# A spectral mixing kernel rewritten: d folded at its half-sample centre, the first inverse stage on 32-row array tiles, products left unsummed, one explicit order list

## The chip, the cores and the metric

The kernel runs on one core of one Trainium2 chip. The metric is the device time of one execution in microseconds (us). Each variant was timed in rounds beside the kernel before on the same chip. An execution is called slow when it is more than 1.5% above the fastest one of the same kernel, and "unknown" when there is only one. Engines are named as in the profile: PE multiplies matrices (PEld is its weight load), DVE, ACT and POOL work elementwise, SP only issues transfers. A queue is named after the engine that issues on it.

## The reference, cut to what matters

```python
x = A_x                                              # [1, 2048, 1024], bfloat16
g = sigmoid((x * gate_w).sum(-1, keepdims=True))
a = irfft2(rfft2(x) * (A_w_r + 1j * A_w_i))          # over both axes
b = irfft2(rfft2(x) * (B_w_r + 1j * B_w_i))
return g * a + (1 - g) * b                           # a, b rounded to bfloat16 first
```

Both kernels compute the transforms as matrix products. The sequence axis is split as s = 16*s2 + s1, with 16 values of s1 and 128 of s2. The stages:

- F1 transforms over s2, F2 over d, F3 over s1. The work then falls into 16 units: eight for even columns of the spectrum, eight for odd ones.
- cmul multiplies a unit by the two complex weights.
- I1 is the inverse over s1. Its result is copied from PSUM (the memory that PE writes its results to) into a tile `rl` in SBUF (the on-chip memory that holds all other tiles).
- A **shuffle** moves `rl` by DMA into the exchange buffer `re` (even) or `ro` (odd). It turns pieces that lie on different partitions into long rows on few partitions. It is a transfer from SBUF to SBUF, and no engine can do I2 until all units of its parity have been shuffled.
- I2 (with the gate folded into its weights) and I3 finish the inverse; the even half is kept as `ev` and added to and subtracted from the odd half.

## The kernel before: the parts that matter

```python
def cmul(n):                         # DVE: two products of 2064 columns, then two sums
    ...
    nc.vector.tensor_tensor(p[:, :, :, 0:M], xb, w[:, :, :, 0:M], ALU.mult)      # for r in 0, 1
    ...
    nc.vector.tensor_tensor(Y[:, 0, :, 0:M], p1[:, :, 0, 0:M], p2[:, :, 1, 0:M], ALU.subtract)
    nc.vector.tensor_tensor(Y[:, 1, :, 0:M], p1[:, :, 1, 0:M], p2[:, :, 0, 0:M], ALU.add)

def i1(n, r):                        # PE: 64-row tiles, one PSUM tile per r
    ...
    for k in range(2):
        w = ((0, 2), (1, 0))[r][k]
        for tt in range(2):
            for jh in range(2):
                hin = hp(jh ^ tt)
                nc.tensor.matmul(ps[hp(jh), tt * 512:(tt + 1) * 512], lhsT=WI[hin, 2 * u + tt, w, :],
                                 rhs=Y[hin, k, 2 * tt:2 * tt + 2, o:o + 256], start=(k == 0), stop=(k == 1))
    ...                              # rl has 4 buffers
    nc.scalar.copy(out=rl[:, :, r, :], in_=ps[:].rearrange("p (t m) -> p t m", t=2))
    if r == 1:
        for tt in range(2):          # the shuffle: 128 partitions -> 8 partitions, 256 KB
            t = 2 * u + tt
            p0 = 32 * (t // 4) + t % 4
            nc.gpsimd.dma_start(RR[par][p0:p0 + 29:4, :, :], rl[:, tt].rearrange("p r m -> p (r m)"))
```

All 32 shuffles go on the POOL queue, which carries nothing else. The main loop issues F2 of unit n, I1 of unit n-3, F3 and cmul of unit n-1, and lets I2 and I3 of the even half begin in its last turns.

Of the kernel before, what the change touches and what calls it, by code (L numbers as in the profile page):

```python
# [20 lines left out]
WID = (257, 256)  # L21
PIT = (258, 256)
# [25 lines left out]

def make_constants():
# [3 lines left out]
    E = np.zeros((NT, 2, 2, 2, 128))  # L53
    EZ = np.zeros((NT, 2, 2, 2, 128))
    for t in range(NT):
        for j, k2 in enumerate(quad_reps(t)):
            th = 2 * np.pi * s2 * k2 / 128
            F[:, t, j // 2, 0, j % 2] = np.cos(th)
            F[:, t, j // 2, 1, j % 2] = -np.sin(th)
            E[t, j // 2, 0, j % 2] = np.cos(th)  # L60
            E[t, j // 2, 1, j % 2] = np.sin(th)
            EZ[t, j // 2, 0, j % 2] = 2 * np.cos(th)
            EZ[t, j // 2, 1, j % 2] = -2 * np.sin(th)
            if k2 == 0:
                F[:, t, j // 2, 1, j % 2] = np.cos(np.pi * s2)
                E[t, j // 2, 1, j % 2] = np.cos(np.pi * s2)
                EZ[t, j // 2, 0, j % 2] = 1
                EZ[t, j // 2, 1, j % 2] = np.cos(np.pi * s2)
    F = F.reshape(128, 128)
    c["F1"] = _bf16np(np.concatenate([F, -F], axis=1))  # L70
    c["E"] = _bf16np(E.reshape(4, 4, 8, 128).transpose(0, 2, 1, 3).reshape(128, 128))
    c["EZ"] = _bf16np(EZ.reshape(128, 128) / 128)
    d1 = np.arange(512)
    i = np.arange(256)
    FD = np.zeros((512, 2, 2, 256))
    IG = np.zeros((2, 2, 256, 512))
    for eo in range(2):
        m = 2 * i + eo
        ph = 2 * np.pi * np.outer(d1, m) / D
        FD[:, eo, 0] = np.cos(ph)  # L80
        IG[eo, 0] = 2 * np.cos(ph).T
        if eo == 0:
            IG[0, 0, 0] = 1
        m = 2 * i + (2 if eo == 0 else 1)
        ph = 2 * np.pi * np.outer(d1, m) / D
        FD[:, eo, 1] = -np.sin(ph)
        IG[eo, 1] = -2 * np.sin(ph).T
        if eo == 0:
            FD[:, 0, 1, 255] = np.cos(np.pi * d1)
            IG[0, 1, 255] = np.cos(np.pi * d1)  # L90
    IG /= S * D
    c["FD"] = _bf16np(FD.reshape(4, 128, 2, 512).transpose(1, 2, 0, 3))
    c["IG"] = _bf16np(IG.reshape(2, 2, 2, 128, 512).transpose(3, 0, 1, 2, 4).reshape(128, 8, 512))
    s1 = np.arange(NS1)
    WF = np.zeros((128, NT, 3, 64))
    WI = np.zeros((128, NT, 3, 64))
    for t in range(NT):
        for jh in range(2):
# [4 lines left out]
            for p in range(64):  # L103
                w = np.exp(-2j * np.pi * k[p] * s1 / S)
                kk = k[p] % 128
                if kk in (0, 64):
                    cc = 0 if kk == 0 else 1
                    al[:, cc, 0, p] = w
                    be[cc, 0, :, p] = w.conj()
                    continue  # L110
                eps = 1 if kk in reps else -1
                j = reps.index(kk if eps > 0 else 128 - kk)
                al[:, 0, j, p] = w
                al[:, 1, j, p] = 1j * eps * w
                be[0, j, :, p] = w.conj()
                be[1, j, :, p] = 1j * eps * w.conj()
            al = al.reshape(64, 64)
            be = be.reshape(64, 64).T
            h = slice(64 * jh, 64 * jh + 64)
            WF[h, t, 0], WF[h, t, 1], WF[h, t, 2] = al.real, al.imag, -al.imag  # L120
            h = h if t % 2 == 0 else slice(64 - 64 * jh, 128 - 64 * jh)
            WI[h, t, 0], WI[h, t, 1], WI[h, t, 2] = be.real, be.imag, -be.imag
    c["WF"] = _bf16np(WF)
    c["WI"] = _bf16np(WI)
# [4 lines left out]
def gated_mix(ctx, tc, x_in, we_in, wo_in, gw_in, out):  # L129
# [3 lines left out]
    xv = x_in.flatten_outer_dims().rearrange("(s2 s1) d -> s2 s1 d", s1=NS1)  # L133
# [5 lines left out]
    wp = ctx.enter_context(tc.tile_pool(name="wp", bufs=1))  # L139
    wk = ctx.enter_context(tc.tile_pool(name="wk", bufs=2))  # L140
    pp = ctx.enter_context(tc.tile_pool(name="pp", bufs=3, space=bass.MemoryType.PSUM))
    pl_pool = tc.alloc_tile_pool(name="plp", bufs=1, space=bass.MemoryType.PSUM)
# [4 lines left out]
    def ptile():  # L147
        return pp.tile([P, 1024], F32, name="pt", tag="pt")

    ctx.enter_context(tc.manual_schedule())  # L150
    warm = const.tile([P, 512], BF16, name="warm")
    nc.vector.memset(warm[:], 0.0)
    wps = ptile()
    for _ in range(6):
        nc.tensor.matmul(wps[:, 0:512], lhsT=warm[:, 0:128], rhs=warm[:], start=True, stop=True)  # L155
    F1 = const.tile([P, 2, 128], BF16, name="f1")
    nc.scalar.dma_start(F1[:].rearrange("p a b -> p (a b)"), dr["F1"])
    gws = const.tile([P, 8], BF16, name="gws")
    nc.scalar.dma_start(gws[:], gw_in)
    Re = big.tile([P, 16 * 1024], BF16, name="re")  # L160
    Ro = big.tile([P, 16 * 1024], BF16, name="ro")
    x = Re[:].rearrange("p (s d) -> p s d", s=NS1)
    for s0, n in ((0, 1), (1, 1), (2, 2), (4, 2), (6, 2), (8, 2), (10, 2), (12, 2), (14, 2)):
        nc.sync.dma_start(x[:, s0:s0 + n, :], xv[:, s0:s0 + n, :])
    FD = const.tile([P, 2, 4, 512], BF16, name="fd")
    WF = const.tile([P, NT, 3, 64], BF16, name="wf")
    WI = const.tile([P, NT, 3, 64], BF16, name="wi")
    IG = const.tile([P, 8, 512], BF16, name="ig")
    Ec = const.tile([P, 128], BF16, name="ec")
    Ez = const.tile([P, 128], BF16, name="ez")  # L170

    y = big.tile([P, 4, 2, 2 * NT, NS1, 4], BF16, name="y")
    Ws = {}
    wt = [wp.tile([P, 2064], BF16, name=f"w{k}", tag=f"w{k}") for k in range(4)]

    def load_w(n):
        par, u = n // NU, n % NU
        if n < 4 or 8 <= n < 12:
            w = wt[n % 4][:]
        elif n < 8:  # L180
            w = Ro[:, (n - 4) * 2064:(n - 3) * 2064]
        else:
            w = y[:, n - 12, 0].rearrange("p t s c -> p (t s c)")
        w = w[:, 0:8 * PIT[par]].rearrange("p (t a m) -> p t a m", t=2, a=4)
        nc.sync.dma_start(w, w_in[par][u])
        Ws[n] = w

    nc.sync.dma_start(FD[:, 0], dr["FD"][:, 0])
    nc.sync.dma_start(WF[:, 0:4], dr["WF"][:, 0:4])
    load_w(0)  # L190
    nc.sync.dma_start(Ez[:], dr["EZ"])
    nc.sync.dma_start(WI[:, 0:4], dr["WI"][:, 0:4])
    load_w(1)
    nc.sync.dma_start(WF[:, 4:16], dr["WF"][:, 4:16])
    load_w(2)
    nc.sync.dma_start(WI[:, 4:16], dr["WI"][:, 4:16])
    nc.sync.dma_start(Ec[:], dr["E"])
    for n in range(3, 8):
        load_w(n)
    nc.sync.dma_start(FD[:, 1], dr["FD"][:, 1])  # L200
    nc.sync.dma_start(IG[:], dr["IG"])

    gwz = const.tile([P, 8, 32], BF16, name="gwz")
    nc.gpsimd.memset(gwz[:], 0.0)
    gh = const.tile([P, 8], F32, name="gh")
    junk = const.tile([P, 8], F32, name="junk")
    nc.scalar.activation(junk[:], gwz[:, 0, 0:8], ACT.Sigmoid)
    nc.vector.tensor_scalar(gh[:], gws[:], 0.5, None, ALU.mult)
    gq = gwz[:].rearrange("p (q e) c -> p q e c", e=2)
    nc.vector.tensor_tensor(gq[:, :, 0, 0], gh[:, 0:4], gh[:, 4:8], ALU.add)  # L210
    nc.vector.tensor_tensor(gq[:, :, 1, 0], gh[:, 0:4], gh[:, 4:8], ALU.subtract)

    yo = y[:].rearrange("p q e t s c -> p (q e t) s c")
    for s1 in range(NS1):
        ps = ptile()
        for q in range(4):
            for h in range(2):
                nc.tensor.matmul(ps[:, q * 256:(q + 1) * 256],  # L218
                                 lhsT=x[:, s1, h * 512 + q * 128:h * 512 + (q + 1) * 128],
                                 rhs=(bc(F1[:, 0, :]).to_broadcast([P, 2, 128]) if h == 0 else F1[:]), start=(h == 0), stop=(h == 1))  # L220
        i_ = ps[:].rearrange("p (a c) -> p a c", c=4)
        if s1 == 15:
            for e, cp in ((0, nc.scalar.copy), (1, nc.vector.tensor_copy)):
                cp(out=y[:, :, e, :, s1, :], in_=ps[:].rearrange("p (q e t c) -> p q e t c", q=4, e=2, c=4)[:, :, e])
        elif s1 % 2 == 1:
            nc.vector.tensor_copy(out=yo[:, :, s1, :], in_=i_)  # L226
        else:
            nc.scalar.copy(out=yo[:, :, s1, :], in_=i_)  # L228

    RR = [r[:].rearrange("p (s f) -> p s f", s=NS1) for r in (Re, Ro)]  # L230
    EV = Re[:].bitcast(F32).rearrange("p (s f) -> p s f", s=NS1)
    EA = const.tile([P, NS1, 128], BF16, name="ea")
    EB = const.tile([P, NS1, 128], BF16, name="eb")
    zt = const.tile([P, NS1], BF16, name="zt")

    def gate_hat():
        ps = ptile()
        for e in range(2):
            for q in range(4):
# [154 lines left out]
    for n in range(12):  # L394
        f2(n)
        if n == 0:
            gate_hat()
# [89 lines left out]
```

## Time and profile before

The median of the runs beside the changed kernel was 145.0 us (144.06 to 148.08 in 4 runs).

| | PE | DVE | ACT | POOL | granted PE clock |
|---|---|---|---|---|---|
| busy us of 144.4 | 121.9 | 97.6 | 93.3 | 19.6 | 0.961 |

Busy time of each engine by stretch (start:end, length, then busy time of PE, PEld, DVE, ACT, POOL, PE clock, DMA share, GB/s):

```profile
42.00:69.00 27.00, 23.57 (x279) 10.90 (x276) 26.14 (x33) 25.81 (x28) 8.06 (x14) 1.00 0.94 241
102.00:136.20 34.20, 32.40 (x300) 20.60 (x302) 21.01 (x20) 15.06 (x16) 2.37 (x4) 1.00 0.33 114
```

The mixed stage is held by DVE and ACT (26.14 and 25.81 of 27 us), the last one by PE (32.40 of 34.20 us).

### The profile page before, as it was taken

To read this page: it belongs to the slowest core of one execution; us is meant where nothing else is said; L and a number is where in the kernel's file an instruction comes from. 1 tells how busy PE (TensorE), PEld (TensorE's weight loads), DVE (VectorE), ACT (ScalarE), POOL (GpSimd) and SP (SyncE) were. 2 spreads that over 40 slices of the span, in tenths; PEclk is the share of its full clock that TensorE was granted. 3 is DMA by queue.
4 is the path that set the end of the run, shared out by engine and by line. 5 is a ranking of instruction groups with operands and counts; after the bars stand their busy time and mean duration, and the time that the engine had idled before them with its cause. 6 is when DMAs were issued, how large, how long until landed. Compare 5 with 4: busy or idle time off the path is not lost.

```text
span 144.4 us, 2878 instructions
## 1 busy us (share of the span) xinstructions
PE 121.9 (84%) x1188; PEld 68.1 (47%) x1206; DVE 97.6 (68%) x113; ACT 93.3 (65%) x97; POOL 19.6 (14%) x37
## 2 busy tenths in 40 slices
PE   6999979929899898888867999868869999999910
PEld 2688844416344443334324345433455665756500
DVE  0177740089279999999999279599433456898990
ACT  4255546665699999999995899997935244253200
POOL 1000000000033222233333033033330000000000
PEclk9999999975799999999999999999999999999985
DMA  4999999968716999999865315527464000464553
GB/s 148 298 361 419 406 411 405 415 244 284 297 14 168 240 279 278 353 250 202 163 139 133 126 18 140 131 43 168 110 166 110 0 0 0 167 253 166 208 228 145
DMA packets 11088, 29.19 MB, mean 202 GB/s; under 512 B 3781, under 2 KB 4165, under 8 KB 10949
## 3 DMA queue, kind: packets, MB, share of 16 engines
q1 hardware_dynamic: 6048, 20.55, 38.3%
q0 software_dynamic: 4608, 8.41, 24.8%
q8 instruction: 9, 0.15, 0.5%
q10 hardware_dynamic: 420, 0.07, 0.3%
q14 instruction: 3, 0.02, 0.0%
HBM read 16.42 MB, written 4.19 MB: 143 GB/s over the span
## 4 chain that ended last, share of the span: by engine, by line
PE 55%; ACT 24%; DMA 9%; issue 4%; DVE 2%; another core or an unknown queue 2%; DVEq 1%; POOL 0%; ACTq 0%; POOLq 0%
PE pt L378 18%; PE pt L218 10%; PE pt L275 10%; ACT rl L349 10%; PE pv L367 9%; DMA re<-rl 5%; DMA zt<-zs 4%; ACT X L310 4%; ACT T L279 3%; PE pt L344 3%; ACT V L370 2%; PE pt L155 2%; ACT zs L245 2%; DVE ot L390 2%
## 5 line engine op out<-in xcount | busy, mean ns | idle before, releaser
L275 PE MATMUL pt<-fd,y 128*128 128x512 bf16 x117 | 30.5, 394 | 3.8 <-ACT rl L349 2.6
L349 ACT CAST rl<-pt 128x1024 bf16<-128x1024 f32 x32 | 32.9, 1038 | 0.0
L378 PE MATMUL pt<-ig,V 128*128 128x512 bf16 x121 | 29.6, 379 | 1.1 <-ACT V L370 0.7
L370 ACT CAST V<-pv 128x1024 bf16<-128x1024 f32 x16 | 16.3, 1021 | 19.2 <-PE pv L367 19.2
L344 PE MATMUL pt<-Y,wi 64*64 64x512 bf16 x256 | 20.1, 387 | 3.8 <-ACT T L279 0.8
L275 PEld LDWEIGHTS <-y 128*128 128x128 bf16 x128 | 12.6, 100 | 20.3 <-issue 8.6
L279 ACT CAST T<-pt 128x1024 bf16<-128x1024 f32 x16 | 16.3, 1017 | 8.3 <-PE pt L275 4.1
L378 PEld LDWEIGHTS <-V 128*128 128x128 bf16 x128 | 11.7, 98 | 13.9 <-ACT V L370 1.9
L354 POOL DMA_DIRECT2D re<-rl x16 | 9.6, 606 | 59.8 <-ACT rl L349 59.8
L310 ACT CAST X<-pt 128x1024 bf16<-128x1024 f32 x16 | 16.5, 1033 | 0.0
L218 PE MATMUL pt<-f_84,re 128*128 128x256 bf16 x128 | 15.6, 289 | 0.0
L218 PEld LDWEIGHTS <-re 128*128 128x128 bf16 x128 | 13.0, 103 | 3.1 <-DMA re<-in_x_dram 0.8
L228 ACT CAST y<-pt 128x1024 bf16<-128x1024 f32 x8 | 8.1, 1013 | 8.4 <-PE pt L218 8.4
L354 POOL DMA_DIRECT2D ro<-rl x16 | 9.5, 596 | 26.4 <-ACT rl L349 26.4
L386 DVE COPY re<-pt 128x1024 f32<-128x1024 f32 x5 | 6.1, 1225 | 10.2 <-PE pt L378 10.2
L226 DVE CAST y<-pt 128x1024 bf16<-128x1024 f32 x7 | 8.6, 1225 | 5.2 <-PE pt L218 5.2
L344 PEld LDWEIGHTS <-wi 64*64 64x64 bf16 x256 | 6.4, 106 | 11.9 <-issue 10.7
L389 DVE TENSOR_TENSOR ot<-pt,re 128x1024 bf16<-128x1024 f32 x8 | 9.8, 1224 | 3.0 <-PE pt L378 3.0
L367 PE MATMUL pv<-ea,re 128*128 128x128 bf16 x64 | 8.1, 219 | 2.9 <-DMA re<-rl 1.7
L295 PE MATMUL pt<-T,wf 64*64 64x512 bf16 (+2 forms) x192 | 9.8, 307 | 0.4 <-ACT T L279 0.3
L367 PEld LDWEIGHTS <-re 128*128 128x128 bf16 x128 | 7.5, 98 | 5.4 <-issue 2.5
L390 DVE TENSOR_TENSOR ot<-re,pt 128x1024 bf16<-128x1024 f32 x8 | 9.7, 1210 | 0.0
(96 smaller groups left out, 128.2 us busy)
## 6 DMA issues: line engine op xcount, KB each, us to landing
re<-rl POOLq DMA_DIRECT2D x16, 256.0 KB, 8.0
ro<-rl POOLq DMA_DIRECT2D x16, 256.0 KB, 5.1
out_dram<-ot SPq DMA_DIRECT2D x8, 512.0 KB, 2.6
re<-in_x_dram SPq DMA_DIRECT2D x7, 512.0 KB, 8.6
ro<-in_we_dram SPq DMA_DIRECT2D x4, 516.0 KB, 8.0
y<-in_wo_dram SPq DMA_DIRECT2D x4, 512.0 KB, 6.5
fd<-cst_fd SPq DMA_DIRECT2D x2, 512.0 KB, 9.1
ig<-cst_ig SPq DMA_DIRECT2D x1, 1024.0 KB
```

The source lines that it names most:

```text
L218: nc.tensor.matmul(ps[:, q * 256:(q + 1) * 256], lhsT=x[:, s1, h * 512 + q * 128:h * 512 + (q + 1) * 128], rhs=(bc(F1[:, 0, :]).to_broadca ...
L275: nc.tensor.matmul(ps[:, tt * 512:(tt + 1) * 512], lhsT=y[:, q, par, 2 * t:2 * t + 2, :, :].rearrange("p j s c -> p (j s c)"), rhs=FD[:, p ...
L279: nc.scalar.copy(out=T[:].rearrange("p a b -> p (a b)"), in_=ps[:])
L295: nc.tensor.matmul(ps[ho, tt * 512 + dst:tt * 512 + dst + ln], lhsT=WF[hp(jh), 2 * u + tt, w, :], rhs=T[hp(jh), tt, src:src + ln], start=( ...
L310: nc.scalar.copy(out=xo, in_=ps[:].rearrange("p (t r m) -> p t r m", t=2, r=2))
L344: nc.tensor.matmul(ps[hp(jh), tt * 512:(tt + 1) * 512], lhsT=WI[hin, 2 * u + tt, w, :], rhs=Y[hin, k, 2 * tt:2 * tt + 2, o:o + 256], start ...
L349: nc.scalar.copy(out=rl[:, :, r, :], in_=ps[:].rearrange("p (t m) -> p t m", t=2))
L354: nc.gpsimd.dma_start(RR[par][p0:p0 + 29:4, :, :], rl[:, tt].rearrange("p r m -> p (r m)"))
L367: nc.tensor.matmul(ps[:, s * 512 + ch * 128:s * 512 + ch * 128 + 128], lhsT=RR[par][:, s1, c0 + 256 * ab:c0 + 256 * ab + 128], rhs=Ew[:, s ...
L370: nc.scalar.copy(out=V[:].rearrange("p s c k -> p (s c k)"), in_=ps[:])
L378: nc.tensor.matmul(ps[:, s * 512:(s + 1) * 512], lhsT=V[:, s, ch, :], rhs=IG[:, par * 4 + ch, :], start=(ch == 0), stop=(ch == 3))
L390: nc.vector.tensor_tensor(ot[:, :, 1, :], ev, pv, ALU.subtract)
```

## The change

The intent: halve the columns of F2 by folding d about its half-sample centre (columns j and 1023-j), take two DVE sums per unit away by letting I1 add up all four products, spread copies over the engines, and give every engine a fixed instruction order. The diff replaces almost the whole kernel. Its core, with cuts marked:

```diff
 # F1: instead of one eviction, a copy and two folds per s1
-    nc.scalar.copy(out=yo[:, :, s1, :], in_=i_)
+    cp(e, t..., ps[:, 512:1024]...)                                  # ACT
+    for v, op in enumerate((ALU.add, ALU.subtract)):                  # DVE, or POOL for eight
+        Q[e].tensor_tensor(yo[:, v, k:k + n, s1, :], a..., b..., op)
 # F2: half the columns
-    for q in range(4): matmul(ps[:, tt*512:(tt+1)*512], lhsT=y[...], rhs=FD[:, par, q, :])
+    for v in range(2):
+        for b in range(2): matmul(ps[:, tt*512+v*256:tt*512+v*256+256], lhsT=y[...], rhs=FD[:, par, v, b, :])
 # cmul: no sums
-    nc.vector.tensor_tensor(Y[:, 0, ...], p1[...], p2[...], ALU.subtract)
-    nc.vector.tensor_tensor(Y[:, 1, ...], p1[...], p2[...], ALU.add)
 # I1: 32 input rows per tile; row groups j of 32 go to separate PSUM banks
+    mm = [(0,0,0,lo,256), (64,1,1,lo,256), (128,0,1,lo,256), (128,1,0,lo,256)]   # even units: 4 tiny ones more
+    for q, (w, ri, wi, a, b) in enumerate(mm):
+        for tt in range(2):
+            for H in range(2):
+                for j in range(2):
+                    r = slice(64*H + 32*j, 64*H + 32*j + 32)
+                    lh = C["WJ"][r, 2*u + tt, w:w + 64]
+                    o = pss[tt][hp(H ^ tt), j*512:(j+1)*512]...
+                    nc.tensor.matmul(o[:, :, a:b], lhsT=lh, rhs=src[r, ri, wi, tt, :, a:b], ...)
 # shuffle: twice as many, half as large, to 4 partitions each
-    nc.gpsimd.dma_start(RR[par][p0:p0+29:4, :, :], rl[:, tt]...)
+    for j in range(2):
+        Q[q].dma_start((Re, Ro)[par][p0+4*j:p0+4*j+25:8, :], rl[:, tt, j, :])
 # order list (one token an instruction group; H is a shuffle, its last letter the queue, S is SP, P is POOL)
+ ... R:3:1:A W:S:11 H:0:0:S R:1:0:A R:1:1:D F3:5:0 W:S:7 ... H:0:1:P F2:6:3 X:4:A ...
+ ... X:14:A H:15:1:P J:12:0:1 VC:0:5:A ... H:13:1:P ... H:12:0:S VC:0:4:A H:15:0:S J:14:0:1 H:12:1:P ...
 # also: eleven rl evictions and some others on DVE, three of the sixteen I3 groups (two even, one odd) in half, POOL fixes column 0
```

I1 sums over 32 rows at a time, so the two row groups j are different outputs. The diff puts them in two PSUM banks of the same 64 partitions. A unit's `rl` therefore holds, on its partitions, 4 exchange rows x 32 pieces (16 values of s1, real and imaginary) instead of 8 rows x 16 pieces. The same 8.4 MB are now moved by 64 shuffles of 128 KB to 4 partitions each, in runs of 1 KB, instead of 32 of 256 KB to 8 partitions, in runs of 2 KB. Half of them go on the SP queue.

## The prediction, as it was put on record

> What bounds the kernel now. No engine bounds the whole span; the page's totals are PE 121.9 us, DVE 97.6, ACT 93.3, POOL 19.6 of 144.4. By windows four stages differ. To 18.6 us the forward transform over s2 streams on PE. From 18.6 to 42 us the pipeline fills badly: DVE is busy 10.2 of 23.4 us, the chain of waits goes through the gate (2.3 us zs copy, 5.8 us zt transfer), and the PE clock falls to 0.66 in 30:40. From 42 to 69 us DVE is 97% and ACT 96% busy. From 102 to 136.2 us PE is 95% busy with I2 (16 matmuls, 0.89 us) and I3 (8 matmuls, 1.73 us).
>
> Removed.
> 1. Half of F2: 128 matmuls of 512 columns (8 take 1.89 us in the chain) become 256 columns: estimate 30 -> 14 us of PE.
> 2. The two sums of cmul: 32 DVE operations of 0.69 us, 22 us. I1 now accumulates the four products on PE.
> 3. Half of I3 for three of sixteen units, 2.6 us of PE.
>
> Added.
> 1. A fold at F1: instead of 16 evictions of 1.0 to 1.2 us, ACT copies to SBUF and DVE (or POOL, for eight) adds and subtracts. From 0.69 us for 512 and 1.22 us for 1024 elements I estimate 0.43 us for 256; DVE pays 32 of them, 13.7 us. Eight odd halves fold on PE (+3.5 us).
> 2. I1 in 32-row tiles: the same 2048 streamed columns per unit, but 32 matmuls instead of 16; even units add 32 tiny ones. Before, 8 matmuls on 64-row tiles took 0.56 us and 8 one-column ones 0.21 us. If eight concurrent tiles stream like four, I1 costs 18 + 7 us. This is the least certain term.
> 3. Eleven rl, three V, two T and two X evictions move to DVE; fixes, folds and odd sums go to POOL. The Trainium skill, "GPSIMD Engine Reference", section "Performance versus the Vector engine", puts a two-input POOL add at about twice the VectorE time (4497 against 2293 ns for 2048 elements); nothing in before checks it.
>
> Sums (estimates, counts times these durations): PE about 107, DVE 104, ACT 89. ACT plus DVE stays near 191: the 22 us saved are spent on the fold. So the gain is PE work and overlap. Even halves of F1 come first, so F2, F3 and products should start near 14 to 18 us; more even I2/I3 units fill PE in the mixed stage. After the last I1, before still has 12 I2 and 13 I3 groups and an 8 us tail (42 us); after has 10 I2, 7 whole and 3 half I3, 24 us, plus some 8 us of bubble and tail.
>
> By stage: 17 us of F1, 72 us mixed, 32 us last: 121; with stalls 123 us. It should be 115 to 132. Chances: faster by over 2% 0.95, within 2% 0.03, slower 0.02. Nearly all of it is critical, since the chain alternates between engines.
>
> What would show it. Page: PE near 107, DVE 104, ACT 89. Groups: F2 near 0.11 us per matmul streamed, no sums after the products, folds near 0.43 us. Windows: DVE over 80% busy from 20 to 45 us, clock at 1.0; about 32 us after the last rl eviction. The zt transfer no longer in the chain.
>
> What would make it wrong. If 32-row tiles don't run concurrently, I1 costs up to twice as much: +15 us. If DVE's products hold up POOL (the skill's "SBUF — State Buffer" says the two share a port pair, exclusively), fixes and shuffles come late and I1 waits. A strict order with four fixed PSUM buffers may stall every engine on one late copy. The odd shuffles may leave a bubble over 5 us before the last stage.

## More of the kernel before

Weight loads and stores go on the SP queue.

The page of the profiled execution begins with busy time per engine, then shows the span in 40 slices of 3.6 us (a digit is the busy share in tenths):

```profile
span 144.4 us, 2878 instructions
PE 121.9 (84%) x1188; PEld 68.1 (47%) x1206; DVE 97.6 (68%) x113; ACT 93.3 (65%) x97; POOL 19.6 (14%) x37
...
PE   6999979929899898888867999868869999999910
DVE  0177740089279999999999279599433456898990
...
PEclk9999999975799999999999999999999999999985
...
L275 PE MATMUL pt<-fd,y 128*128 128x512 bf16 x117 | 30.5, 394 | 3.8 <-ACT rl L349 2.6
L344 PE MATMUL pt<-Y,wi 64*64 64x512 bf16 x256 | 20.1, 387 | 3.8 <-ACT T L279 0.8
...
re<-rl POOLq DMA_DIRECT2D x16, 256.0 KB, 8.0
ro<-rl POOLq DMA_DIRECT2D x16, 256.0 KB, 5.1
```

In the group lines the numbers are busy time, the mean of one instruction in ns, and idle time just before with what ended most of it. L275 is F2, L344 is I1. The last two lines are the shuffles: 256 KB each, 8.0 and 5.1 us in the median from issue to landing.

PE has one longer gap, near 30 us (the digit 2 in its row), and otherwise only short ones.

## The result, and the profile after

The result is correct and slower: 170.8 us in the median (169.52 to 172.66 in 4 runs) against 145.0 us. The ratio is 1.175 (95% interval 1.161 to 1.189). Ratios in this document are the mean time of one kernel's fast runs over that of the other's fast runs of the same rounds, so not quite the ratio of the medians quoted. The page after:

```profile
span 169.7 us, 4270 instructions
PE 120.6 (71%) x1814; PEld 81.9 (48%) x1814; DVE 99.7 (59%) x119; ACT 82.7 (49%) x104; POOL 56.2 (33%) x85
...
PE   7499999959895396733303998999702779999710
DVE  0558849777939839602820097796002416879791
...
PEclk9969999999999569995555699999965558999995
...
L507 PE MATMUL pt<-p,wj 32*64 32x510 bf16 (+2 forms) x768 | 22.2, 338 | 10.1 <-ACT rl L208 4.6
...
L436 PE MATMUL pt<-fd,y 128*128 128x256 bf16 x128 | 16.8, 282 | 2.0 <-DVE rl L210 2.0
...
re<-rl POOLq DMA_DIRECT2D x16, 128.0 KB, 8.2
...
ro<-rl POOLq DMA_DIRECT2D x16, 128.0 KB, 8.3
```

Set against the lines of before: of the three engines costed only PE has more work than was predicted, and no engine's is near the span. F2 (L436) has fallen from 30.5 to 16.8 us. I1 (L507) takes 22.2 us for all units. But a shuffle of half the size now lands in 8.2 or 8.3 us, and PE has holes: five slices in the middle with digits 3, 3, 3, 0 and 3, and two later with 0 and 2. The granted clock falls to 0.5 in and after those holes, so part of PE's 120.6 us is work at a lower clock. The windows of the holes, columns as above:

```profile
70.00:80.00 10.00, 3.91 (x60) 1.81 (x60) 2.39 (x3) 5.15 (x6) 1.37 (x2) 0.81 0.71 154
80.00:90.00 10.00, 1.50 (x24) 0.44 (x23) 5.30 (x5) 2.02 (x2) 2.73 (x4) 0.50 0.81 210
...
120.00:130.00 10.00, 1.86 (x16) 0.66 (x8) 1.23 (x1) 1.52 (x2) 0.38 (x1) 0.70 0.46 116
```

In these 30 us PE works 7.3 us. The other engines idle for most of it too. What they wait for (engine, line, what it waited for: us in total, times, longest):

```profile
ACT rl L208 <- DMA re<-rl: 10.4, 3, 4.3
...
DVE rl L210 <- DMA ro<-rl: 10.3, 1, 10.3
...
ACT rl L208 <- DMA ro<-rl: 8.8, 1, 8.8
...
DVE p L479 <- DMA wx<-in_wo_dram: 7.6, 1, 7.6
...
PE pt L533 <- DMA ig<-cst_ig: 8.4, 1, 8.4
```

Copies into `rl` wait for shuffles out of `rl` (its four buffers are all in transit), products wait for a weight load, and the first I2 (L533) waits for a transfer. The profile puts that last wait down to the load of the `ig` table, which I2 does not read. By the trace's packet records (my own count) the table's last packet ended at 94.3 us, after I2 had begun at 91.8; the last 1 KB packet of the even shuffles on SP ended at 90.1 us, and the semaphore of that shuffle was complete at 91.2. I2 waited for the shuffles. The SP queue's own timeline shows why (start, length, instruction, count):

```profile
44.27 17.88 SPq L522 DMA_DIRECT2D re<-rl  x8
62.26 2.93 SPq L278 DMA_DIRECT2D y<-in_wo_dram  x1
65.23 0.89 SPq L278 DMA_DIRECT2D wx<-in_wo_dram  x1
66.22 14.69 SPq L522 DMA_DIRECT2D re<-rl  x6
80.96 1.31 SPq L266 DMA_DIRECT2D ig<-cst_ig  x1
82.32 1.61 SPq L278 DMA_DIRECT2D y<-in_wo_dram  x3
98.11 32.53 SPq L522 DMA_DIRECT2D ro<-rl  x16
```

The lengths of rows with several shuffles hold the waits between them too. The six from 66.22 us stand back to back and take 14.69 us, 2.4 us for each 128 KB. One issue alone takes 0.53 us when little is on its way on SP, and up to 6.24 us when several transfers are. What holds it the profile does not name. It is not the transfer eight before, for which each issue has to wait in this program: by the landings in the trace, that one had landed at least 2.6 us before each issue of over 1 us after 40 us began. The weight loads stand in line among them: `wx` at 65 us, for which DVE waits 7.6 us, and the last three at 82 us.

I counted the packet records of this trace and of a variant of the kernel before with its shuffles on SP (e4_before_sp below). Where the 4-row shuffles run alone on SP, 4.3 packets of 1 KB are in flight, 46 ns each, so about 90 GB/s. With 8-row shuffles at most 8.3 packets of 2 KB are in flight, 84 ns each, so about 200 GB/s. The size of the packets is not what makes the difference: 1 KB in 46 ns and 2 KB in 84 ns are nearly the same rate. All this is on SP. On POOL the packets are of 4 KB in all kernels that I counted, and no limit of four shows: with several shuffles outstanding, 4-row ones have 6 to 9 packets in flight (e1 below, stretches of 3 us after 72 us), 8-row ones 7 to 12 (e13 below).

The figures on SP are what the Trainium skill says to expect: the page "DMA: Bandwidth & Descriptors", section "Why a DMA increments its semaphore by 16 and not by 1", states that a transfer is given the largest number of DMA engines, up to 16, that divides the size of the slowest dimension on both sides. Four destination rows allow four engines, eight rows eight. The traces agree with it on SP, at 4.3 and 8.3 packets in flight; for POOL no run here shows it. The prediction did not use it.

### The profile page after: what moved, and what is told of

Its sections match the earlier page's. It is cut to its first block, busy times and chain, and to the rows that moved or that the text cites. A ratio compares the mean times of both kernels' runs of the same rounds, so it can differ in the third digit from the quotient of the medians.

```text
span 169.7 us, 4270 instructions
## 1 busy us (share of the span) xinstructions
PE 120.6 (71%) x1814; PEld 81.9 (48%) x1814; DVE 99.7 (59%) x119; ACT 82.7 (49%) x104; POOL 56.2 (33%) x85
## 5 line engine op out<-in xcount | busy, mean ns | idle before, releaser
L208 ACT CAST rl<-pt 128x1024 bf16<-128x1024 f32 x21 | 20.8, 1017 | 25.7 <-DMA re<-rl 10.4
L507 PE MATMUL pt<-p,wj 32*64 32x510 bf16 (+2 forms) x768 | 22.2, 338 | 10.1 <-ACT rl L208 4.6
L210 DVE CAST rl<-pt 128x1024 bf16<-128x1024 f32 x11 | 13.4, 1223 | 25.6 <-PE pt L507 14.0
L208 ACT CAST V<-pt 128x1024 bf16<-128x1024 f32 x13 | 13.2, 1016 | 25.7 <-PE pt L533 25.7
L533 PE MATMUL pt<-ea,re 128*128 128x128 bf16 x64 | 11.1, 266 | 18.8 <-ACT re L208 9.1
L479 DVE TENSOR_TENSOR p<-X,ro 128x2048 bf16<-128x2048 bf16 x16 | 20.1, 1302 | 5.8 <-DMA ro<-in_we_dram 2.9
L507 PEld LDWEIGHTS <-wj 32*64 32x64 bf16 x768 | 12.3, 111 | 18.8 <-issue 16.0
L533 PEld LDWEIGHTS <-re 128*128 128x128 bf16 x128 | 10.2, 123 | 21.5 <-issue 9.9
L377 POOL TENSOR_TENSOR y<-wx 128x256 bf16<-128x256 f32 x16 | 14.1, 908 | 15.8 <-ACT wx L208 8.8
L436 PE MATMUL pt<-fd,y 128*128 128x256 bf16 x128 | 16.8, 282 | 2.0 <-DVE rl L210 2.0
L208 ACT COPY wx<-pt 128x256 f32<-128x256 f32 (+1 forms) x25 | 11.3, 459 | 14.1 <-PE pt L332 8.6
L332 PE MATMUL pt<-f,re 128*128 128x128 bf16 x192 | 14.3, 237 | 2.6 <-DMA re<-in_x_dram 2.4
L436 PEld LDWEIGHTS <-y 128*128 128x128 bf16 x128 | 12.1, 100 | 5.5 <-issue 4.0
```

The lines of the kernel that those rows point to most:

```text
L208: nc.scalar.copy(out=out, in_=in_)
L210: Q[e].tensor_copy(out=out, in_=in_)
L332: nc.tensor.matmul(o, lhsT=lh, rhs=rh, start=(h == 0), stop=(h == 1))
L377: Q[e].tensor_tensor(yo[:, v, k:k + n, s1, :], a.rearrange("p (k c) -> p k c", c=4), b.rearrange("p (k c) -> p k c", c=4), op)
L436: nc.tensor.matmul(ps[:, tt * 512 + v * 256:tt * 512 + v * 256 + 256], lhsT=y[:, v, par, b, 2 * t:2 * t + 2, :, :].rearrange("p j s c -> p ...
L479: nc.vector.tensor_tensor(p[:, r], xb, w, ALU.mult)
```

## The experiments

Theories, in the order in which they came up:

- **A**: the SP queue is what hurts; shuffles there are slow and hold up the loads.
- **B**: too few `rl` buffers.
- **C**: too many transfers, whatever their form.
- **D**: the strict order list stalls the engines on each other, whatever the transfers do.
- **E**: a burst of weight loads takes the DMA bandwidth from the shuffles.
- **F**: the form of the shuffle (4 rows, 1 KB runs) that the 32-row tiling brings makes it slow on either queue, worse on SP.

B could not be tried alone, as more `rl` buffers did not fit into SBUF. Two others could not be built: one shuffle for both row groups, and one with 16 pieces as the slowest dimension of both sides, which by the rule above would have put 16 engines to work with all else kept.

### All shuffles on one queue

e1_all_pool puts all 64 on POOL, e2_all_sp all on SP:

```diff
-... H:0:0:S ... H:3:0:S ... H:15:0:S ...
+... H:0:0:P ... H:3:0:P ... H:15:0:P ...      # e1; e2 has :S for all
```

> Edit: the 32 shuffles that stand on the SP queue go to the POOL queue; nothing else moves. Theory A (the SP queue carries a shuffle with 4 destination partitions on only about 4 of 16 DMA engines, 88 packets of 1 KB per us, so each takes 1.5 to 2 us of a queue that also carries the weights and the I3 table): the idle stretches at 73 to 92 us and 121 to 130 us go, the time falls to 128 to 140 us. Rival B (four rl buffers are too few for a landing of 8 us, on any queue): the POOL landings are 8 us as well, so 160 us or more. Rival C (halved shuffles, 64 of 128 KB in place of 32 of 256 KB, are too many transfers): with all 64 on one software queue, 170 us or more.

> Edit: all 64 shuffles on the SP queue, which doubles the suspected cost. Theory A: 64 shuffles of 128 packets at 88 packets per us are 93 us of transfer in series, between about 40 us and the last 30 us of work, so 185 to 210 us. Rivals B and C: near 170 us.

Measured: e1 163.78 us (161.44 to 165.34, two fast and two slow), ratio to before 1.109 (1.095 to 1.123); e2 186.99 us (one run, state unknown). Both correct. So the SP queue does cost: some 16 us more with all on it, and 7 us (by medians) to 10 us (by ratios to before) less with none. But most of the loss stays without it, and A, which foretold 128 to 140 us, is only part of the answer. The forecast that e1 meets is B's (160 us or more); but too few buffers and too slow a landing are the same wait, which this run does not separate. e1's POOL queue has waits of its own (profile of a slow run, 164.4 us; start, length, instruction, count, idle before and what ended it):

```profile
65.26 0.69 POOL L522 DMA_DIRECT2D re<-rl  x1 [1.69 <-DMA re<-rl]
67.81 0.69 POOL L522 DMA_DIRECT2D re<-rl  x1 [1.86 <-DMA re<-rl]
70.20 0.69 POOL L522 DMA_DIRECT2D re<-rl  x1 [1.69 <-DMA re<-rl]
```

Here each does wait for the shuffle eight before it, which by the trace had landed 0.3 to 0.6 us before (at 65.0, 67.3 and 69.9 us): one issue per 2.4 us, with POOL's fixes for I1 behind them. There are six such waits, 10.1 us in all. With 32 shuffles of 256 KB on POOL, in the kernel before and in e13 below, there are none.

### One row per transfer

e3_row_dmas cuts every shuffle on SP into four of one row, 32 KB, to give the parts to the queue separately:

```diff
-        Q[q].dma_start((Re, Ro)[par][p0+4*j:p0+4*j+25:8, :], rl[:, tt, j, :])
+        for i in range(4):                                   # on SP only
+            Q[q].dma_start((Re, Ro)[par][p0+4*j+8*i:p0+4*j+8*i+1, :], rl[32*i:32*i+32, tt, j, :])
```

> Edit: the 32 shuffles stay on the SP queue, but each is issued as four, one per destination partition, with 32 pieces of 1 KB outermost: same bytes, same packets, four times as many transfers (128). Theory A with its mechanism (the outermost count of 4 confines a transfer to 4 engines): packets in flight rise from 4.3 to about 16, the stalls go, 128 to 142 us, the DMA share rises where shuffles run alone. If it is the SP queue as such (issue cost per transfer, in order), not the engine count: more transfers make it worse, 180 us or more. Rival C too: worse than 170 us.

Measured: 191.52 us (190.63 to 192.69), ratio 1.309 (1.297 to 1.322), correct. This run did not test what it was made for. SP became the limit by issuing:

```profile
105.19 44.94 SPq L524 DMA_DIRECT2D ro<-rl  x57
```

That is 0.79 us per transfer with the waits between them (one issue takes 0.59 us in the median), with about 3 packets in flight by my count. What follows is only that cutting transfers smaller is worse; it says nothing about the number of DMA engines.

### The shuffles' bytes taken away

e7_tiny_shuffle keeps every instruction and its order but moves 4 KB in each shuffle instead of 128 KB. Its output is wrong, which doesn't matter for the time.

```diff
-        Q[q].dma_start((Re, Ro)[par][p0+4*j:p0+4*j+25:8, :], rl[:, tt, j, :])
+        Q[q].dma_start((Re, Ro)[par][p0+4*j:p0+4*j+25:8, 0:512], rl[0:97:32, tt, j, :])
```

> Edit to the changed kernel: every shuffle stays where it is, on its queue, but moves 4 KB (one 1 KB piece to each of its 4 partitions) instead of 128 KB; the result is wrong on purpose. Theory A' (moving the shuffles' bytes to 4 partitions a time is what the lost time is): the stalls at rl, V and the late loads go and the time is 120 to 133 us, near the prediction. Rival D (the strict order list over four PSUM buffers stalls the engines by itself, whatever the transfers do): 150 us or more.

Measured: 130.42 us (130.03 to 130.72), ratio 0.891 (0.884 to 0.898). From the page of this run:

```profile
PE 110.6 (86%) x1814; PEld 75.3 (58%) x1814; DVE 99.6 (77%) x119; ACT 81.8 (63%) x104; POOL 53.1 (41%) x85
...
PE   6969999999779799779989989999969999996500
...
PEclk9999999999999999999999999999999999999995
```

No holes, a full clock, and a time inside the predicted range (115 to 132). So D falls as a cause by itself: with the same order list and the same 64 transfers, what costs 40 us (170.8 against 130.4) is what the shuffles carry, and how. PE's busy time falls by 10 us because the clock stays up. C, as a matter of the bare count, falls too.

### The loads as rivals

e8_pool_tinyloads is e1 with the last four weight loads cut to 1/16 (wrong); e9_pool_loads_act is e1 with the late loads on the ACT queue.

```diff
 # e8
-        Q[q].dma_start(w, w_in[n // NU][n % NU])
+        Q[q].dma_start(w[:, 0:128], w_in[n // NU][n % NU][:, 0:128])        # for n >= 12
 # e9
-... W:S:10 ... W:S:11 ... W:S:9 ... W:S:15 ... c:S:IG ...
+... W:A:10 ... W:A:11 ... W:A:9 ... W:A:15 ... c:A:IG ...
```

> Edit to the kernel with all shuffles on POOL: the last four weight loads move 32 KB instead of 512 KB (wrong result on purpose), which takes 2 MB from the burst at 47 to 70 us. Theory E (with the SP queue freed, these loads go out in one burst and the shuffles wait behind them in the DMA engines): 142 to 155 us, the shuffles' median landing well below 7.1 us. If the burst is no matter: 160 us or more.

> Edit to the kernel with all shuffles on POOL: the eight late weight loads and the I3 table are issued from the ACT queue at their places in the order list, so that they are spread in time again instead of going out together. Theory E: 145 to 157 us. If contention with loads is no matter: 160 us or more.

Measured: e8 159.79 us and e9 173.55 us, one run each, state unknown, where e1 took 163.78 (161.44 and 163.17 in its fast runs). The bytes of those four loads are worth 4 us at most, and spreading loads to ACT made it worse. This does not rule E out as a part of e1's loss: in e8 too the DMA engines are full from 50 to 60 us (share 1.05) while PE works 2.51 of 10 us. E falls as the main cause because e13 below, with all of these loads and the shuffles on POOL, takes 149.66 us: its DMA engines are as full (share 0.99 from 45 to 66 us), and PE still works 16.05 of these 21 us.

### The kernel before with the shuffles' form and queue changed

Three kernels put one property of the new shuffles into the old kernel. e4_before_sp only changes the queue. e10_before_split cuts each 8-row shuffle into two of 4 rows, 128 KB, one unit half on SP and one on POOL, as the changed kernel has them. e11_before_split_pool has the same cut, all on POOL.

```diff
 # e4
-                nc.gpsimd.dma_start(RR[par][p0:p0+29:4, :, :], rl[:, tt]...)
+                nc.sync.dma_start(RR[par][p0:p0+29:4, :, :], rl[:, tt]...)
 # e10 (e11: nc.gpsimd for both)
-                nc.gpsimd.dma_start(RR[par][p0:p0+29:4, :, :], rl[:, tt]...)
+                for h in range(2):
+                    (nc.sync, nc.gpsimd)[tt].dma_start(RR[par][p0+16*h:p0+16*h+13:4, :, :], rl[64*h:64*h+64, tt]...)
```

> Edit to the kernel before: its 32 shuffles (8 destination partitions, 256 KB, runs of 2 KB) move from the POOL to the SP queue, behind and between the loads. If the SP queue's in-order issue is what hurts, in any kernel: 152 to 175 us. If only the four-partition form does: within 3% of the kernel before.

> Edit to the kernel before: each of its 32 shuffles of 256 KB to 8 partitions becomes two of 128 KB to 4 partitions; those of one half of each unit stand on the SP queue, the others on POOL, as in the changed kernel. Nothing else of the change is in it. Theory F (a shuffle to 4 partitions runs on only 4 DMA engines, so it lands late and holds its rl buffer and its queue, whatever the compute around it): 155 us or more. Rival G (the loss needs the changed kernel's order list or its other transfers): within 3% of the kernel before.

> The same split of the kernel before with all 64 halves on the POOL queue. Theory F: 150 to 165 us, landings of 6 us or more for 128 KB in the quiet odd stage, where 256 KB took 5.1 us. Rival G: within 3%.

| shuffles in the kernel before | us | before, same rounds | |
|---|---|---|---|
| 8 rows, SP (e4) | 147.88, one run | 146.16 | +1.2% |
| 4 rows, POOL (e11) | 150.94, one run | 147.17 | +2.6% |
| 4 rows, half SP, half POOL (e10) | 156.67, its one fast run of four | 147.17 | +6.5% |

All are correct. Three of e10's four runs were slow (160.98 to 163.1 us) and are left out of the table. Neither the SP queue alone nor the 4-row form alone hurts the old kernel much; together they cost it some 10 us, by one fast run. And it gets the same hole as the changed kernel, here in a window and in the wait that ends it (the profile is of a slow run, 160.98 us):

```profile
80.00:90.00 10.00, 1.61 (x16) 1.64 (x17) 2.15 (x3) 0.00 (x0) 0.91 (x2) 0.52 0.50 160
...
PE pv L369 <- DMA ro<-rl: 12.5, 1, 12.5
```

The profile names an odd shuffle as what ended the wait, again by the last event. By the trace the last even shuffle on SP landed at 87.7 us, 0.7 us before I2 began at 88.4. Before that, SP did wait for the transfer eight before: seven issues in a row, from 71.09 to 84.52 us, began within 0.1 us of its landing. e10's pieces are of 4 rows with runs of 2 KB, and on SP at most 4.2 of them are in flight, so it is the 4 rows and not the shorter runs that make a shuffle slow there. For POOL e11 decides nothing: 150.94 us lies in F's range (150 to 165) and in the rival's (within 3%). Its landing times are a miss of my expectation, as the median of the odd ones is 4.5 us and not 6 or more; POOL waited for earlier shuffles eight times, 11.0 us in all, where it never does in the kernel before.

### The changed kernel with 8-row shuffles

e12_eight_rows keeps the whole rewrite but gives I1 32 x 32 tiles: real and imaginary go to separate banks, the row groups j to separate partitions. Then `rl` again holds 8 rows, and one 256 KB shuffle replaces two. e13_eight_rows_pool has all 32 on POOL.

```diff
-                        lh = C["WJ"][r, 2*u + tt, w:w + 64]
-                        o = pss[tt][hp(H ^ tt), j*512:(j+1)*512]...
+                            lh = C["WJ"][r, 2*u + tt, w:w + 32]              # one pass per c (re, im)
+                            q0 = 64*(H ^ tt) + 32*j
+                            o = pss[tt][q0:q0+32, c*512:(c+1)*512]...
...
-        for j in range(2):
-            Q[q].dma_start((Re, Ro)[par][p0+4*j:p0+4*j+25:8, :], rl[:, tt, j, :])
+        Q[q].dma_start((Re, Ro)[par][p0:p0+29:4, :], rl[:, tt].rearrange("p j m -> p (j m)"))
```

> Edit to the changed kernel: I1 runs on 32-row by 32-column array tiles, real and imaginary parts in separate PSUM banks, so that one half unit again fills 8 rows by 16 samples and is shuffled in one transfer of 256 KB to 8 partitions, on the same queue and place as before (32 transfers instead of 64); everything else stays. PE pays: 64 matmuls of 512 columns per odd unit instead of 32. Theory F: 132 to 150 us, at most 8.3 packets in flight where SP shuffles run alone, and PE becomes the limit again. Rival: the 4-row form is not what costs, so 168 us or more, as PE work only grew.

> The same with all 32 shuffles on the POOL queue. Theory F: 132 to 150 us, near the run with both queues; a quiet-stage landing near 5 us as in the kernel before.

Measured: e12 149.33 us (147.91 to 149.76), ratio 1.013 (1.004 to 1.022), neither faster nor slower by 2%; e13 149.66 us (one run). Both correct. With 8 rows the queue no longer matters, and 21 us of the loss are gone, although PE has more to do:

```profile
PE 126.3 (86%) x2318; PEld 83.4 (57%) x2326; DVE 99.6 (68%) x119; ACT 82.7 (56%) x104; POOL 43.7 (30%) x69
...
L511 PE MATMUL pt<-p,wj 32*32 32x510 bf16 (+2 forms) x1280 | 34.6, 343 | 3.2 <-issue 1.3
...
re<-rl POOLq DMA_DIRECT2D x8, 256.0 KB, 5.9
```

A shuffle twice as large lands in 5.9 us where it took 8.2. I1 costs 34.6 us instead of 22.2. This shows that the form of the shuffle (F) is what costs most, and what was against changing it: the form that makes the shuffle quick makes I1 slow. e12 changes three things of the form at once, 8 rows for 4, runs of 2 KB for 1 KB and 32 transfers for 64. Against the number alone speaks e7 (64 transfers, 130.42 us), against the runs alone e10.

e17_eight_rows_tiny takes the bytes of e12's shuffles away (16 KB each, wrong), to split what is left:

```diff
-        Q[q].dma_start((Re, Ro)[par][p0:p0+29:4, :], rl[:, tt].rearrange("p j m -> p (j m)"))
+        Q[q].dma_start((Re, Ro)[par][p0:p0+29:4, 0:1024], rl[0:113:16, tt].rearrange("p j m -> p (j m)"))
```

> Edit to the version with 32x32 tiles and 8-row shuffles: each shuffle moves 16 KB instead of 256 KB (wrong result on purpose). If the PE work of those tiles is what holds that version at 149 us: 142 to 149 us. If the shuffles still cost: 130 to 138 us.

Measured: 139.06 us, one run, between the two forecasts: both costs are there. Of the 19 us between e12 and e7, about 9 us (139.1 - 130.4) go with the form of I1, and about 10 us (149.3 - 139.1) with the bytes of 8-row shuffles.

### The unsummed products undone

e14_summed keeps the rewrite but sums the products on DVE again, in place, so that I1 can run on 64-row tiles with 8-row shuffles. e15_summed_act also moves eight `rl` copies from DVE to ACT.

```diff
+    def sums(n):
+        p = Ps[int(n)][:].rearrange("p r t (a w) m -> p r w (t a) m", w=2)
+        for k, op in ((0, ALU.subtract), (1, ALU.add)):
+            nc.vector.tensor_tensor(p[:, 0, k], p[:, 0, k], p[:, 1, 1 - k], op)
...
-                            lh = C["WJ"][r, 2*u + tt, w:w + 32]
+                        ... lhsT=C["WJ"][hp(H), 2*u + tt, w:w + 64], rhs=src[hp(H), ri, wi, tt, :, a:b]
 # e15 besides
-... R:0:0:D ... R:3:0:D ... R:5:0:D ...
+... R:0:0:A ... R:3:0:A ... R:5:0:A ...
```

> Edit to the changed kernel: I1's part of the change is undone and all the rest kept: the products are summed on DVE again (in place, 32 operations of 0.69 us, +22 us of DVE), I1 runs on 64-row tiles with 16 matmuls per unit, and so each shuffle is one of 256 KB to 8 partitions; same order list. If the 4-row shuffle forced by the 32-row tiles is what failed: 135 to 146 us, DVE near 121 us busy and the limit. If something else in the rewrite costs: 155 us or more.

> The same, with 8 of the 11 rl evictions that the order list gives to DVE moved to ACT (DVE about 112 us, ACT about 91). If DVE is the limit there: 3 to 8 us less than without. If the strict order or PE is: the same within 2%.

Measured: e14 152.4 us (151.23 to 153.22), ratio 1.054 (1.037 to 1.071), between its two forecasts; e15 154.93 us (152.52 to 156.87; one fast run, 152.52, and three slow), no gain and a miss. Both correct. Now DVE binds: 120.6 us busy in e14, and full over 50 us:

```profile
30.00:80.00 50.00, 35.52 (x549) 22.37 (x546) 48.03 (x56) 32.82 (x36) 18.52 (x27) 0.85 0.59 172
```

So, for all units at once, leaving the products unsummed was worth having (e12 has 1.013): the fold has taken the room on DVE that the sums would need. For the odd units alone this is not shown: the mixture below has sums there and came out no slower, but changes the order list too.

### A mixture

e18_mixed runs even units as in e12 and odd units as in e14, with the last I1 ahead of two even I3 groups. e19_mixed_act also moves three odd `rl` copies and one V copy from DVE to ACT.

```diff
 # e18
+    even units: 32 x 32 tiles, products unsummed; odd units: sums on DVE, 64-row tiles
-... U:0:5:2 R:12:1:A H:12:0:S VC:0:4:A H:15:0:S J:14:0:1 H:12:1:P U:0:4:3 R:14:0:A R:14:1:D E:5:A H:14:0:S H:14:1:P ...
+... the same without U:0:5 and U:0:4, which now stand after the last J and H
 # e19 besides
-... R:11:0:D ... R:8:1:D ... VC:0:3:D ... R:13:1:D ...
+... R:11:0:A ... R:8:1:A ... VC:0:3:A ... R:13:1:A ...
```

> Edit to the changed kernel: 8-row shuffles for all units; even units as in the 32x32 version, odd units with summed products on 64-row tiles (DVE +11 us, PE about -7 us against the 32x32 version), and the I1 of the last unit ahead of two even I3 groups. From 149 us of the 32x32 version: 7 us less if PE's I1 work sets the odd stage's pace, 2 to 3 us less for the filled bubble: 139 to 146 us. If DVE takes over as the limit in the odd stage: 147 to 151 us.

> The same, with three odd rl evictions and one V eviction moved from DVE to ACT. If DVE limits the odd stage: 1 to 4 us less than without; otherwise the same within 2%.

Measured: e18 149.92 us (144.9 to 153.15; one fast run, 144.9, three slow). e19 143.09 us (two fast, 141.91 and 141.96; two slow, 144.21 and 146.32). Both correct. The kernel before, in the same rounds, had one fast run of 143.48 us and six slow ones (145.86 to 147.81). e19 is the best version found: fast against fast it is 1% quicker, median against median 2%. That is not enough to call it faster.

## Why the prediction was wrong

**Right: the busy sums.** PE was predicted at 107 us, and is 110.6 in e7, where the clock is full (120.6 after, where it is not). DVE: predicted 104, measured 99.7. ACT: predicted 89, measured 82.7. F2: predicted 14 us, measured 16.8 busy. The fold: predicted 0.43 us, measured 417 ns in the mean of DVE's 32. I1: "the least certain term", predicted 25 us and named as the first danger, measured 22.2 us. The 32-row tiles do run side by side: 32 matmuls of 512 columns took 1.07 us in one odd unit.

**Right, but of no use: POOL's cost.** Following the Trainium skill ("GPSIMD Engine Reference", section "Performance versus the Vector engine") the prediction put a POOL add at about twice DVE's. For 256 elements the trace has 720 to 733 ns in 13 of POOL's 16 folds, against 415 ns on DVE in the median: 1.75 times; the operands differ, as DVE reads one from PSUM. The other three took 1685 to 1708 ns, each beside a product on DVE, which brings POOL's mean to 908. In e7 POOL was busy for 41% of the span.

**The step that failed: "121; with stalls 123 us", and with it "Nearly all of it is critical".** The sum by stage contained the engines' work and 8 us "of bubble and tail", taken from the kernel before. It contained no term for the shuffles. They were written down only as a danger: "The odd shuffles may leave a bubble over 5 us before the last stage". The diff had changed their number, their size, their destination rows and the queue of half of them, and none of that was costed, though the diff shows it and the trace of before has their landing times, and one of them, 6.53 us long, in its chain of waits at 69.90 us. The missing term measures 40 us (170.8 in the changed kernel, 130.4 in e7).

**What that term consists of.** The steps are measured, one change at a time where it could be had. They ran on different chips, on which the kernel before took 145.0 to 147.2 us in the median, so a difference of 2 us between two rows means nothing; e1's 163.8 has two slow runs in it (fast: 161.4 and 163.2):

| step | us |
|---|---|
| changed kernel | 170.8 |
| all shuffles on POOL (e1) | 163.8 |
| 8 rows instead of 4, half on SP (e12; I1 costs more PE) | 149.3 |
| 8 rows, bytes taken away (e17, one run) | 139.1 |
| 4-row form of I1, bytes taken away (e7) | 130.4 |

The mechanism, as far as it is shown: the 32-row tiling without sums leaves 4 rows on `rl`'s partitions; on SP a transfer to 4 rows has about half as many packets in flight as one to 8 (4.3 against 8.3); 128 KB then land 1.4 to 1.6 us apart where SP's shuffles run alone (98 to 109 us) and are issued 2.4 us apart in the mixed stage; the four `rl` buffers stay occupied, so copies, then I1, then products wait; weight loads queue behind the shuffles; I2 starts late; in the holes the granted clock falls, which adds some 10 us of PE time. e10 shows the 4-row form hurting the kernel before, e12 shows that the changed kernel recovers without it.

**Wrong in what would make it wrong.** Of the four dangers named, tiles that don't run concurrently and the strict order by itself did not come true at any size that e7 would show. POOL held up by DVE did come true, but small: the three slow folds above, 1 us each, and the same three in e7. The fourth was the right one, put at 5 us.

**What stays open.** How the 40 us divide between the SP queue's four engines and the waits on POOL is not settled: e1 still takes 163.8 us with nothing on SP, while the same cut on POOL costs the kernel before only 2.6% (e11). POOL's other work is hardly the reason: of its 34 us in e1 (77.9 us busy less 44 us of issuing) only the fixes, 3.9 us at most, stand among the shuffles. e1's trace has two other candidates, the six waits for the shuffle eight before (10.1 us) and the weight loads, which then fill the DMA engines from 50 to 70 us (share 1.02 and 1.06); no run separates them. Nor is it tested why the 4-row form costs the kernel before some 10 us (e10) and the changed kernel 21 us or more (e12). e2, e4, e8, e9, e11, e13 and e17 are single runs of unknown state. The 7 us between the prediction and e7 were not pursued.

## What to carry to other kernels

When a change retiles a matrix product, follow its output one stage further: which partitions hold which rows decides the shape of the next transfer, and going back from 4 rows to 8 won 21 us here, although it made the matrix product itself slower. Cost every transfer whose size, number, rows or queue a diff changes, from its landing time in the trace, before adding up engines. And when busy sums come out as predicted but the time does not, shrink the transfers' bytes with all instructions kept: one such run (e7) separated 40 us of transfers from everything else.

## What the Trainium skill lacked or had wrong

- "DMA: Bandwidth & Descriptors", section "Why a DMA increments its semaphore by 16 and not by 1", has the rule for the number of engines, and the traces agree on SP (4.3 and 8.3 packets in flight). No page has a figure for a transfer inside SBUF to few partitions: 128 KB to 4 rows landed in 8.2 us from POOL in a busy stage, and 1.4 to 1.6 us apart on SP alone; 256 KB to 8 rows landed in 5.9 us from POOL.
- The same page, section "Rules for kernel authors", says that spreading transfers over issuing engines does not help. For 8-row shuffles that agrees (149.33 and 149.66 us). For 4-row shuffles the choice of queue moved the time from 163.8 (all POOL) over 170.8 (half) to 187.0 us (all SP), so it is not neutral there, which this line does not foretell.
- "TensorEngine Tiling (Array Packing)", section "Performance Considerations", says when to tile and that the copies out of PSUM may become the limit. It does not warn that the tile shape settles which partitions the output lands on, and so the next transfer. Here 32-row tiles with 64 columns took 22.2 us but led to 4-row shuffles, 32 x 32 tiles took 34.6 us and led to 8-row ones, and the kernel with the slower tiles was 21 us quicker.
- No page has a measured stream of small transfers on SP: 57 one-row transfers of 32 KB took 44.94 us, 0.79 us each with the waits, and one issue took 0.59 us in the median.
- "GPSIMD Engine Reference", section "Performance versus the Vector engine", has its ratio for 2048 elements (1.96). At 256 elements it was 725 against 415 ns in the median, 1.75 times, with one of DVE's operands in PSUM; beside DVE's products POOL took 1685 to 1708 ns.
